# Relu² attention and a ReGLU feed-forward: another order for the loads and the attention pieces of the first two batches, a lag of 8 slots, and a one-piece last copy

## The chip, the cores and the metric

The kernel runs on one core of a Trainium2 chip. The metric is the device time of the kernel in microseconds (us). The time before is 423.1 us, the median of 4 runs (422.57 to 424.98).

## The reference

Inputs are q, k, v of shape (8, 12, 448, 64), w_gate and w_val of (768, 1536) and w_out of (1536, 768), all float32; the output has 3584 rows (8 batches of 448 tokens) of 768 columns, float32.

```python
scores = scale * np.matmul(q, k.transpose(0, 1, 3, 2))
attn = np.maximum(scores, 0.0) ** 2 / S
attn_out = np.matmul(attn, v)
x = attn_out.transpose(0, 2, 1, 3).reshape(B * S, H * D)
gate = np.maximum(x @ w_gate, 0.0)
val = x @ w_val
out = gate * val @ w_out
```

## The kernel before

**Data.** Every load is a DMA that POOL (GpSimd) issues (L329, in `dma_in`); it turns float32 into bf16 on the way, and all products are bf16 with float32 sums. The weights stay in SBUF: w_gate and w_val in six column pieces of 256 (`wg0..5`, `wv0..5`, 384 KB each as bf16), w_out in two column halves (`wo0`, `wo1`, 1152 KB each). The list LOADS (L906) sets the order of the loads of batches 0 and 1 and of all weights. In it `k0404` means k of batch 0 from head 4 on, 4 heads; `a` and `b` are the last 3 and the first 4 of the seven row tiles of q; `q` is both; `v` is v; `I` makes the identity matrix; `g3` is wg3 and wv3; `o1` is wo1. POOL issues a load only when the load eight places before it has landed, by the planner's reckoning.

**Attention.** For batches 0 and 1 q and k are turned on TensorE (`turn`, L444; transposes L460 into `t_ps`, copied to `qkT` by VectorE or ScalarE, L466 and L468). From batch 2 on the DMA transposes them (L501). Heads are taken in three groups of four. A piece of scores is four to eight 64x64 matmuls into `s_ps` (L591, L599 for the odd seventh key tile), then relu on ScalarE or VectorE (L609, L611), the square on VectorE (L628) and the product with v (L649), whose sum is copied to `xT` (L679, L681). Batch 0 is done in two parts of query rows, 192 (A) and then 256 (B), so that work can start early.

**Feed-forward.** For 128 columns of d_ff at a time, a gate product `g_ps` and a value product `v_ps` of six steps of 128 each; ScalarE takes the relu of the gate (L808), VectorE multiplies (L815) and leaves `hT`. Then an output product `o_ps` for 128 tokens and half of the 768 columns, of twelve steps. The first 24 products of batch 0 use the full 128x128 array (L715). All later ones use 64x64 tiles (L725, `Product.piece`): the upper 64 rows of the array (row 0) and the lower 64 (row 1) run side by side, row 1 going over the same products LAG slots later (`chain_ops`, L731; a slot is one step of 64x64 tiles in both rows). Both rows add into one PSUM bank, so the first matmul of row 1 in a product must come after row 0's last of that chunk of six: `ordered` (L434, called in L722) puts a wait on TensorE itself there. Output products are copied out of PSUM (L859 on ScalarE, L861 on VectorE) and stored by SP (L891).

**Order.** A planner (`Planner`, `plan`) goes over the operations with a cost each, keeps a time for each engine and for the load queue (`dmaq`), and at each step emits the operation that can start first. Its times decide only the order in which each engine gets its instructions; on the chip semaphores keep the dependences. For the attention of batch 0 and the turns of it, a list written out by hand, ORDER (L959), stands in for a choice: `T1k` is the turn of k of group 1, `A21` score piece 1 of group 2 of part A, `XA1` and `YA1` the two halves of the product with v, and an `f` puts a piece into two single PSUM banks. Feed-forward products are fitted between. Before the first data, `idle(8)` in `first_zeros` (L954) issues idle matmuls of 128x512 zeros into `w_ps` (L442), and the planner adds more (`filler`, L105 to L117) where it sees a gap before 24 us.

**The end.** The very last half of the output, 64+64 rows by 384 columns, is copied in two pieces of 192 columns, one by ScalarE and one by VectorE (L865 to L867), and then stored by SP (64 rows) and by ScalarE's queue (the other 64).

Of the kernel before, what the change touches and what calls it, by code (L numbers as in the profile page):

```python
# [12 lines left out]
ET = mybir.EngineType  # L13

XBAR_FROM = 2
LAG = 9
CHUNK = 6
NFULL = 24
PACE = 1.3
# [19 lines left out]
class Op:  # L39
    def __init__(self, engs, emit, deps=(), alloc=(), reads=(), xfer=0.0, prio=1, delay=0.0, bias=0.4,  # L40
                 mode=None, late=(), n=0, pace=0.0):
        self.engs, self.emit, self.n = engs, emit, n
        self.pace, self.after, self.anchor, self.name = pace, None, False, None
        self.mode, self.late = mode, list(late)
        self.deps, self.alloc, self.reads = list(deps), list(alloc), list(reads)
        self.xfer, self.prio, self.delay = xfer, prio, delay
        self.bias = bias
        self.lat = 1.3
        self.start = self.end = None


class Planner:
# [4 lines left out]
    AHEAD = 0.1  # L57
    BLOCK, HELD, SKEW = 256, 412, 100
    GROUP, APART = 3, 1.0

    def __init__(self):
        self.t = {"POOL": 1.35}
        self.ops = []
        self.dmaq = 0.0
        self.landed = []
        self.mode = "F"
        self.count, self.fetched = 0, []
# [36 lines left out]
    def commit(self, op, s, e):  # L104
        if e == "PE" and self.filler and 3.0 <= self.t.get(e, 0.0) < 24.0:  # L105
            res, one, make = self.filler
            t = max(self.t[e], min(res.free, default=1e9) + self.LAT)
            one *= 2 if t < 6.0 else 1
            n = int((s - t - 0.35) / one)
            if n > 0:  # L110
                fill = make(n)
                self.mode = fill.mode
                fill.start, fill.eng, fill.end = t, e, t + n * one
                res.free.remove(min(res.free))
                res.free.append(fill.end)
                self.t[e] = fill.end
                self.ops.append(fill)  # L117
        op.start, op.eng = s, e
        d = op.engs[e]
        if e == "PE":  # L120
            if op.mode[0] != self.mode:
                d += self.SWITCH
            self.mode = op.mode[-1]
        if op.n:
            for i in range(op.n):
                self.count += 1
                if (self.count + self.SKEW) % self.BLOCK == 0:
                    t = max([s + d * i / op.n] + self.fetched[-1:])
                    self.fetched.append(t + (6.15 if self.dmaq > t + 4.0 else 2.2))
        self.t[e] = s + d  # L130
        op.end = s + d
        if op.xfer:
            if e == "POOL":
                self.dmaq = max(self.dmaq, op.end + op.lat) + op.xfer
                op.end = self.dmaq + 0.7
                self.landed.append(op.end)
            else:
                op.end += 2.0 + op.xfer
        for b in op.alloc:
            b.res.free.remove(min(b.res.free))  # L140
            b.last = op.end
        for b in op.reads:
            b.readers -= 1
            b.last = max(b.last, op.end)
            if b.readers == 0:
                b.res.free.append(b.last)
        self.ops.append(op)
# [101 lines left out]
def kernel(  # L249
# [28 lines left out]
    OH = d_model // 2  # L278
# [43 lines left out]
        nc.gpsimd.affine_select(out=ident, in_=ident, pattern=[[-1, 128]], compare_op=ALU.is_equal,  # L322
                                fill=0.0, base=0, channel_multiplier=1)

    def dma_in(dst, src, n_desc, kb, deps=(), alloc=(), rate=380.0, pace=0.0):
        def emit():
            if op.after is not None:
                follow(nc.gpsimd.nop().ins, op.after.name, "pace of the loads")
            nc.gpsimd.dma_start(out=dst(), in_=src)  # L329

        op = Op({"POOL": 0.55 + 0.00047 * n_desc + (0.1 if pace else 0.0)}, emit, deps=deps, alloc=alloc, xfer=kb / rate,
                pace=pace)
        op.lat = 0.75 if n_desc <= 128 else 1.3
        pool_ops.append(op)
        return op

# [32 lines left out]
    def load_heads(b, h0, n, what="kv", pace=0.0):  # L369
        if b not in bat:  # L370
            bat[b] = Batch()
            bat[b].buf = Buf(r_in, NT if b >= XBAR_FROM else (3 if b == 0 else 2) * NQ)
            bat[b].vbuf = Buf(r_v, NQ * len(PARTS(b)))
            bat[b].tbuf = Buf(r_xb, NQ * (2 * NC + 1) if b > 0 else NQ * (NC + 1) * len(PARTS(b)))
            bat[b].qk_op, bat[b].v_op = {}, {}
        st = bat[b]

        def tile_of(name, n):
            if not hasattr(st, name):
                setattr(st, name, inp.tile([128, H, n, D], BF16, name=name))  # L380
            return getattr(st, name)

        hs = slice(h0, h0 + n)
        if b < XBAR_FROM:
            pt = lambda x: x[b, hs].rearrange("(a c) (p t) d -> (c p) a t d", c=2, t=NT)
            dst = lambda w, t0, t1: tile_of("qk", NT).rearrange("p (w a) t d -> p w a t d", w=2)[:, w, h0 // 2:(h0 + n) // 2, t0:t1]
            for c, x, w, t0, t1 in (("k", k, 1, 0, NT), ("q", q, 0, 0, NT), ("a", q, 0, 0, QA), ("b", q, 0, QA, NT)):
                if c in what:
                    op = dma_in(lambda w=w, t0=t0, t1=t1: dst(w, t0, t1), pt(x)[:, :, t0:t1], 64 * n, 16 * (t1 - t0) * n, rate=380.0 if b else 300.0,
                                alloc=[st.buf] if h0 == 0 and c == "k" else [])  # L390
                    for h in range(h0, h0 + n):
                        st.qk_op[(c if c != "q" else "a", h)] = op
        else:
            rows = lambda x: x[b, hs].rearrange("h (p t) d -> p h t d", t=NT)
            if "k" in what:
                k_op = dma_in(lambda: tile_of("qk", NT)[64:128, hs], rows(k), 64 * n, 112 * n, rate=340.0, pace=pace,
                              alloc=[st.buf] if h0 == 0 else [])
                q_op = dma_in(lambda: tile_of("qk", NT)[0:64, hs], rows(q), 64 * n, 112 * n, rate=340.0, pace=pace)
                st.qk_op[h0] = (k_op, q_op)
        if "v" in what:  # L400
            for r in range(2):
                src = v[b, hs].rearrange("h (p t) d -> p h t d", t=NT)[:, :, NC * r:NC * r + NC + 1]
                op = dma_in(lambda r=r: tile_of("vv", NC + 1)[64 * r:64 * r + 64, hs], src, 64 * n, 64 * n,
                            alloc=[st.vbuf] if h0 == 0 and r == 0 else [], rate=340.0 if b else 300.0,
                            pace=pace)
                for h in range(h0, h0 + n):
                    st.v_op.setdefault(h, []).append(op)
# [31 lines left out]
    def idle(n):  # L439
        w_ps = bank("w_ps")  # L440
        for _ in range(n):
            nc.tensor.matmul(w_ps, lhsT=zeros[:, :128], rhs=zeros, start=True, stop=True)  # L442
# [288 lines left out]
    def chain_ops(prods):  # L731
# [17 lines left out]
        res = []  # L749
        for c in range(0, n + LAG, six):  # L750
            top = [slots[t] if t < n else None for t in range(c, c + six)]
            low = [slots[t - LAG] if 0 <= t - LAG < n else None for t in range(c, c + six)]
            work = [(u, l) for u, l in zip(top, low) if u or l]
# [75 lines left out]
    def ffn_prods(b):  # L829
# [12 lines left out]
        for ti in tiles:  # L842
# [3 lines left out]
            for hf in range(2):  # L846
# [3 lines left out]
                ps = prod.ps  # L850
# [11 lines left out]

                final = b == B - 1 and ti == 2 * NC
                last_half = final and hf == 1
                pieces = [(0, OH, {"ACT", "DVE"})]  # L865
                if last_half:
                    pieces = [(0, OH // 2, {"ACT"}), (OH // 2, OH // 2, {"DVE"})]  # L867
                if last_half:
                    ps.readers = 2
                done = []  # L870
                for c0, n, engs in pieces:
                    cost = {e: d for e, d in on_psum(n).items() if e in engs}
# [27 lines left out]
                elif hf == 1:  # L900
                    others.append(Op({"SP": 0.2}, lambda f=emit_store: f(0, d_model, both), deps=cps, reads=[obuf],
                                     xfer=1.5))
        return res


    LOADS = ("k0004 a0008 k0404 k0804 a0804 I v0004 b0804 v0804 v0404 b0004 b0404 g0 g1 g2 kqv1004 "  # L906
             "kqv1804 g3 g4 kqv1404 g5 o0 o1")
    for x in LOADS.split():
        if x == "I":
            id_op = Op({"POOL": 0.35}, identity)  # L910
# [42 lines left out]

    def first_zeros():  # L954
        nc.vector.memset(zeros, 0.0)
        idle(8)

    head = {"W": Op({"PE": 3.0}, first_zeros, mode="F", n=16)}
    ORDER = ("W A21f A11 A22f B22 A20f T2k B11f T0a A00 A02f A13f XB1 A01 A10f YA0 B01 B03 YA2 A23 "  # L959
             "XA1f A12f T2a A03f B02 T0k B10 B13 XB2f T0b B00f B21f B12f XA0 T2b XA2 T1k T1a YB0 YB1 "  # L960
             "XB0 YB2 B23 YA1 B20 T1b")
    names = ORDER.split()
    for x in range(NQ):
        for what in "kab":
# [8 lines left out]
    head = [head[x.rstrip("f")] for x in names]  # L973
# [5 lines left out]
    for b in range(1, B):  # L979
        for g in range(NQ):  # L980
            pt = Part(b, g, 0, S)
# [59 lines left out]
```

## Time and profile before

| | us |
|---|---|
| median of 4 runs | 423.1 |
| all runs | 424.98, 422.57, 423.28, 422.93 |
| the profiled execution's own time | 424.98 |
| its span in the profile | 423.3 |
| TensorE matmuls busy | 412.6 |
| ScalarE, VectorE, GpSimd busy | 240.2, 185.4, 72.8 |
| mean granted TensorE clock | 0.999 |

The profile is of one execution, the first of the four. Its times count from the start of the span. PE is TensorE's matmuls, PEld its weight loads, which run beside the matmuls; DVE is VectorE, ACT ScalarE, POOL GpSimd and SP SyncE. A queue with a q after its name (SPq, POOLq) issues DMAs. Matmuls are pipelined, so one that is listed with 0.35 us stands only some 0.05 us behind the one before it, four in a slot of 0.189 us; ends of matmuls are modelled. Where a row ends with `[1.37 <-DMA qk<-in_k_dram]`, the engine stood idle for 1.37 us before it and the load of k ended that.

### The profile page before, as it was taken

To read this page: it belongs to the slowest core of one execution; us is meant where nothing else is said; L and a number is where in the kernel's file an instruction comes from. 1 tells how busy PE (TensorE), PEld (TensorE's weight loads), DVE (VectorE), ACT (ScalarE), POOL (GpSimd) and SP (SyncE) were. 2 spreads that over 40 slices of the span, in tenths; PEclk is the share of its full clock that TensorE was granted. 3 is DMA by queue.
4 is the path that set the end of the run, shared out by engine and by line. 5 is a ranking of instruction groups with operands and counts; after the bars stand their busy time and mean duration, and the time that the engine had idled before them with its cause. 6 is when DMAs were issued, how large, how long until landed. Compare 5 with 4: busy or idle time off the path is not lost.

```text
span 423.3 us, 19116 instructions
## 1 busy us (share of the span) xinstructions
PE 412.6 (97%) x8847; PEld 373.6 (88%) x8847; DVE 185.4 (44%) x340; ACT 240.2 (57%) x362; POOL 72.8 (17%) x118
## 2 busy tenths in 40 slices
PE   7899899999999999999999999999999999999995
PEld 3577569988999889999999999999999999986695
DVE  1975555245632665354535345543533445102200
ACT  3973467457667776755567556774557655332221
POOL 7836510011005102400420122020000000000000
PEclk9999999999999999999999999999999999999999
DMA  8999999798299766959787986297003300040014
GB/s 110 180 199 198 199 205 196 116 152 125 38 141 183 133 81 90 167 120 125 104 114 134 158 118 85 31 155 139 4 2 77 77 3 4 5 111 3 3 41 113
DMA packets 77488, 44.88 MB, mean 106 GB/s; under 512 B 36832, under 2 KB 73952, under 8 KB 77408
## 3 DMA queue, kind: packets, MB, share of 16 engines
q0 software_dynamic: 39360, 24.39, 42.7%
q1 hardware_dynamic: 37968, 19.18, 25.0%
q8 instruction: 69, 1.13, 1.1%
q10 hardware_dynamic: 80, 0.10, 0.1%
q14 instruction: 11, 0.09, 0.1%
HBM read 48.76 MB, written 11.01 MB: 141 GB/s over the span
## 4 chain that ended last, share of the span: by engine, by line
PE 83%; DMA 12%; POOL 3%; issue 0%; DVE 0%; ACT 0%; POOLq 0%
PE o_ps L725 24%; PE v_ps L725 23%; PE g_ps L725 23%; PE s_ps L649 7%; PE s_ps L591 6%; DMA qk<-in_k_dram 5%; DMA wo<-in_moe_w_out_dram 5%; DMA wv<-in_moe_w_val_dram 3%; POOL wg L329 1%; PE s_ps L599 1%; POOL qk L329 1%; POOL wv L329 1%; POOL vv L329 0%; DVE o_sb L861 0%; ACT o_sb L859 0%
## 5 line engine op out<-in xcount | busy, mean ns | idle before, releaser
L725 PE MATMUL g_ps<-xT,wg 64*64 64x448 bf16 x2160 | 205.8, 349 | 0.0
L725 PE MATMUL v_ps<-xT,wv 64*64 64x448 bf16 x2160 | 194.6, 349 | 0.0
L609 ACT ACTIVATE r_sb<-s_ps 128x896 bf16<-128x896 f32 (+4 forms) x173 | 149.8, 882 | 73.6 <-PE s_ps L591 57.8
L725 PE MATMUL o_ps<-wo,hT 64*64 64x384 bf16 x2688 | 146.7, 323 | 0.4 <-DVE qkT L468 0.3
L628 DVE TENSOR_TENSOR at<-r_sb 128x896 bf16<-128x896 bf16 (+3 forms) x163 | 99.8, 617 | 105.2 <-ACT r_sb L609 105.0
L725 PEld LDWEIGHTS <-wg 64*64 64x64 bf16 x2160 | 135.5, 107 | 9.9
L725 PEld LDWEIGHTS <-wv 64*64 64x64 bf16 x2160 | 131.8, 107 | 10.3
L725 PEld LDWEIGHTS <-hT 64*64 64x64 bf16 x2688 | 131.9, 107 | 2.6 <-DMA wo<-in_moe_w_out_dram 0.5
L815 DVE TENSOR_TENSOR hT<-v_ps,g_sb 128x448 bf16<-128x448 f32 (+2 forms) x102 | 60.9, 597 | 101.0 <-PE v_ps L725 91.9
L591 PE MATMUL s_ps<-qkT 64*64 64x448 bf16 (+2 forms) x648 | 82.7, 330 | 0.7 <-ACT r_sb L609 0.5
L808 ACT ACTIVATE g_sb<-g_ps 128x448 bf16<-128x448 f32 (+2 forms) x102 | 53.0, 519 | 51.2 <-PE g_ps L725 44.9
L649 PE MATMUL s_ps<-at,vv 64*64 64x448 bf16 (+2 forms) x672 | 49.5, 339 | 0.2 <-ACT r_sb L609 0.2
L591 PEld LDWEIGHTS <-qkT 64*64 64x64 bf16 x648 | 42.7, 106 | 4.5 <-issue 2.4
L859 ACT ACTIVATE o_sb<-o_ps 128x384 f32<-128x384 f32 (+1 forms) x56 | 27.8, 496 | 23.9 <-PE o_ps L725 23.5
L649 PEld LDWEIGHTS <-vv 64*64 64x64 bf16 x756 | 36.5, 107 | 2.4 <-issue 1.3
L329 POOL DMA_DIRECT2D vv<-in_v_dram x44 | 27.5, 630 | 52.6 <-PE s_ps L649 12.9
L679 ACT CAST xT<-s_ps 128x896 bf16<-128x896 f32 (+2 forms) x24 | 20.8, 865 | 23.4 <-PE s_ps L649 23.2
L922 POOL COPY mark<-qkT 64x1 bf16<-64x1 bf16 x5 | 0.9, 181 | 124.4 <-DMA qkT<-spare 124.4
L329 POOL DMA_DIRECT2D qk<-in_k_dram x24 | 15.6, 649 | 18.0 <-ACT g_sb L808 10.3
L329 POOL DMA_DIRECT2D qk<-in_q_dram x26 | 17.1, 657 | 8.8 <-ACT r_sb L609 3.2
L599 PE MATMUL s_ps<-qkT 64*64 64x448 bf16 (+2 forms) x108 | 16.1, 329 | 0.0
L490 DVE COPY spare<-qk 128x768 bf16<-128x768 bf16 x42 | 12.5, 354 | 0.0
(31 smaller groups left out, 97.5 us busy)
## 6 DMA issues: line engine op xcount, KB each, us to landing
out_dram<-o_sb SPq DMA_DIRECT2D x54, 192.0 KB, 3.5
qk<-in_k_dram POOLq DMA_DIRECT2D x24, 224.0 KB, 5.6
vv<-in_v_dram POOLq DMA_DIRECT2D x42, 128.0 KB, 5.6
qk<-in_q_dram POOLq DMA_DIRECT2D x21, 224.0 KB, 6.0
wg<-in_moe_w_gate_dram POOLq DMA_DIRECT2D x6, 384.0 KB, 10.5
wv<-in_moe_w_val_dram POOLq DMA_DIRECT2D x6, 384.0 KB, 11.1
wo<-in_moe_w_out_dram POOLq DMA_DIRECT2D x2, 1152.0 KB, 16.9
vv<-in_v_dram POOLq DMA_DIRECT2D x2, 384.0 KB, 12.1
```

What stands on the lines that cost most here:

```text
L329: nc.gpsimd.dma_start(out=dst(), in_=src)
L490: nc.vector.tensor_copy(box["p"][:, :, s], st.qk[:, :, t, :].rearrange("p (a c) d -> p a c d", c=2))
L591: nc.tensor.matmul(half_of(h2)[o:o + P2, m * n:(m + 1) * n], lhsT=kq(1, j, h2, key_off(b) + c * 128 + o, P2), rhs=kq(0, j, h2, self.c0, n) ...
L599: nc.tensor.matmul(half_of(u)[o:o + 64, :n], lhsT=kq(1, j, h2, key_tail(b), P2), rhs=kq(0, j, h2, self.c0, n), start=True, stop=True)
L609: o.name = nc.scalar.activation(dst, src, AF.Relu).ins.name
L628: lambda: nc.vector.tensor_tensor(self.at_tile(i), loc["r"][:, :2 * ne], loc["r"][:, :2 * ne], ALU.mult),
L649: ins = nc.tensor.matmul(x_of(slice(64 * h2, 64 * h2 + 64), j), lhsT=st.vv[p, 4 * g + 2 * j + h2, NC * (1 - row) if tail else c + row, :], ...
L679: nc.scalar.copy(dst, src)
L725: ins = nc.tensor.matmul(self.out()[c], lhsT=self.weights(p, k)[:, c], rhs=self.moving(p, k), start=(row == 0 and k == 0), stop=(row == 1 ...
L808: nc.scalar.activation(loc["gs"], gp.out(), AF.Relu)
L815: nc.vector.tensor_tensor(hs["hT"][:, mf, t0:t0 + n], vp.out(), loc["gs"], ALU.mult)
L859: nc.scalar.activation(out=dst, in_=src, func=AF.Copy, scale=float(out_scale))
```

## The change

It does six things:

1. LOADS has another order. Among others, q's last tiles of heads 8–11 come first, v of batch 0 is loaded after all its k, and of batch 1 the heads 8–11 come between wo0 and wo1, where they stood before wg3.
2. ORDER, the hand-written order of the turns, score pieces and v products of the head, is another.
3. The planner's model of the load queue is another: a load is counted as slower by 0.95 us for each instruction block that is fetched while the queue has not run empty, the first 9.2 us go at 0.64 of the rate, and small loads of batch 0 have an allowance (`skew`).
4. LAG is 8, was 9.
5. `idle(WARMUP)` with WARMUP = 7 takes the place of `idle(8)`, and its planned cost of 3.0 becomes 1.25 + 0.425 · 7; the filler's matmuls count double before 4.7 us, not before 6.0.
6. The last half of the last output tile is copied in one piece of 384 columns on VectorE.

```diff
-LAG = 9
+LAG = 8
+WARMUP = 7
...
-            one *= 2 if t < 6.0 else 1
+            one *= 2 if t < self.WARM else 1
...
             if e == "POOL":
-                self.dmaq = max(self.dmaq, op.end + op.lat) + op.xfer
-                op.end = self.dmaq + 0.7
+                if op.end + op.lat > self.dmaq + self.lag:
+                    self.drained = op.end + op.lat
+                t, work = max(self.dmaq, op.end + op.lat), op.xfer
+                slow = min(work, max(0.0, self.COLD - t) * self.COLD_RATE)
+                self.dmaq = t + slow / self.COLD_RATE + work - slow
+                self.lag = 0.95 * sum(1 for f in self.fetched if self.drained < f < self.dmaq)
+                op.end = self.dmaq + self.lag + 0.1 + op.skew
...
-        op = Op({"POOL": 0.55 + 0.00047 * n_desc + (0.1 if pace else 0.0)}, emit, deps=deps, alloc=alloc, xfer=kb / rate,
+        op = Op({"POOL": 0.62 + 0.00045 * n_desc + (0.1 if pace else 0.0)}, emit, deps=deps, alloc=alloc, xfer=kb / rate,
                 pace=pace)
-        op.lat = 0.75 if n_desc <= 128 else 1.3
+        op.lat = 0.75
+        op.skew = skew
...
-                pieces = [(0, OH, {"ACT", "DVE"})]
-                if last_half:
-                    pieces = [(0, OH // 2, {"ACT"}), (OH // 2, OH // 2, {"DVE"})]
-                if last_half:
-                    ps.readers = 2
+                pieces = [(0, OH, {"DVE"} if last_half else {"ACT", "DVE"})]
...
-    LOADS = ("k0004 a0008 k0404 k0804 a0804 I v0004 b0804 v0804 v0404 b0004 b0404 g0 g1 g2 kqv1004 "
-             "kqv1804 g3 g4 kqv1404 g5 o0 o1")
+    LOADS = ("a0804 k0004 I a0004 k0404 a0404 k0804 v0804 v0008 b0804 b0008 g0 g1 kqv1004 g2 g4 "
+             "kqv1404 g3 g5 o0 kqv1804 o1")
...
-        idle(8)
-
-    head = {"W": Op({"PE": 3.0}, first_zeros, mode="F", n=16)}
-    ORDER = ("W A21f A11 A22f B22 A20f T2k B11f T0a A00 A02f A13f XB1 A01 A10f YA0 B01 B03 YA2 A23 "
-             "XA1f A12f T2a A03f B02 T0k B10 B13 XB2f T0b B00f B21f B12f XA0 T2b XA2 T1k T1a YB0 YB1 "
-             "XB0 YB2 B23 YA1 B20 T1b")
+        idle(WARMUP)
+
+    head = {"W": Op({"PE": 1.25 + 0.425 * WARMUP}, first_zeros, mode="F", n=2 * WARMUP)}
+    ORDER = ("W YA0 B22f T1a A21f A20 T0k A10 T2a T0b A03 A01 T0a XA2f B03 B10f A22 XA1 B12 B00f YB0 "
+             "B02f A02 XB1 A11 T2b A12f T1k A23f B23 B13f T2k B21 B11 XA0f B20f YB2 YA2 XB0f XB2 A00f "
+             "A13f T1b YB1 YA1 B01")
```

Both ORDER lists name the same operations; an operation that cannot start yet is passed over for the next that can.

More of the change, by code (lines that the diff above doesn't have):

```diff
@@ L47, in __init__ @@
         self.bias = bias
-        self.lat = 1.3
+        self.lat, self.skew = 1.3, 0.0
         self.start = self.end = None
@@ L59 @@
     GROUP, APART = 3, 1.0
+    COLD, COLD_RATE = 9.2, 0.64
+    WARM = 4.7
     def __init__(self):
@@ L63, in __init__ @@
         self.ops = []
-        self.dmaq = 0.0
+        self.dmaq = self.lag = self.drained = 0.0
         self.landed = []
@@ L323, in identity, with dma_in @@
                                 fill=0.0, base=0, channel_multiplier=1)
-    def dma_in(dst, src, n_desc, kb, deps=(), alloc=(), rate=380.0, pace=0.0):
+    def dma_in(dst, src, n_desc, kb, deps=(), alloc=(), rate=380.0, pace=0.0, skew=0.0):
         def emit():
@@ L388, in load_heads @@
                 if c in what:
-                    op = dma_in(lambda w=w, t0=t0, t1=t1: dst(w, t0, t1), pt(x)[:, :, t0:t1], 64 * n, 16 * (t1 - t0) * n, rate=380.0 if b else 300.0,
+                    op = dma_in(lambda w=w, t0=t0, t1=t1: dst(w, t0, t1), pt(x)[:, :, t0:t1], 64 * n, 16 * (t1 - t0) * n, rate=380.0,
+                                skew=0.8 if b == 0 and t1 - t0 < 4 else 0.0,
                                 alloc=[st.buf] if h0 == 0 and c == "k" else [])
@@ L392, in load_heads @@
                         st.qk_op[(c if c != "q" else "a", h)] = op
+                        if c == "q":
+                            st.qk_op[("b", h)] = op
         else:
@@ L403, in load_heads @@
                 op = dma_in(lambda r=r: tile_of("vv", NC + 1)[64 * r:64 * r + 64, hs], src, 64 * n, 64 * n,
-                            alloc=[st.vbuf] if h0 == 0 and r == 0 else [], rate=340.0 if b else 300.0,
+                            alloc=[st.vbuf] if h0 == 0 and r == 0 else [], rate=340.0 if b > 1 else 380.0,
                             pace=pace)
```

## Prediction

> **What bounds the kernel now.** I read the share of the span and the chain that ended last first, then TensorE's waits, then its rows around each wait.
>
> ```profile
> PE 412.6 (97%) x8847; PEld 373.6 (88%) x8847; DVE 185.4 (44%) x340; ACT 240.2 (57%) x362; POOL 72.8 (17%) x118
> ...
> PE 83%; DMA 12%; POOL 3%; issue 0%; DVE 0%; ACT 0%; POOLq 0%
> ```
>
> TensorE is busy 412.6 of 423.3 us, so about 10.7 us at most are idle, and the chain is TensorE except for a transfer part early. Where that part ends is seen in the chain cut to 30–70 us (columns: start, length, what):
>
> ```profile
> 34.64 12.17 DMA wv<-in_moe_w_val_dram
> 46.81 0.28 issue
> 47.10 19.18 DMA wo<-in_moe_w_out_dram
> 66.27 0.04 issue
> 66.32 0.35 PE o_ps L725 x2
> ```
>
> The last weight load, wo1 (second half of w_out), is issued at 47.10 and lands at 66.3; from there the chain is TensorE alone. By stretches of the profile TensorE is busy 33.68 of 33.70 us from 66.3 to 100, and all of every 100 us to 400. So the end is **66.3 us plus the TensorE work that stands after wo1's first use**. Time won before 66.3 counts only if wo1 lands earlier, or if more work has been put ahead of it. TensorE's waits (us in total, times, longest), matmuls first and weight loads after:
>
> ```profile
> PE t_ps L460 <- DMA qk<-in_k_dram: 2.6, 3, 1.4
> PE w_ps L442 <- DVE zeros L955: 1.3, 1, 1.3
> PE v_ps L715 <- DMA wv<-in_moe_w_val_dram: 0.6, 1, 0.6
> PE s_ps L591 <- ACT r_sb L609: 0.5, 1, 0.5
> ...
> PEld L725 <- DMA wo<-in_moe_w_out_dram: 0.5, 1, 0.5
> ```
>
> TensorE stands only 0.5 us at wo1; the largest wait is 1.4 us for a k load:
>
> ```profile
> 47.94 0.58 PE L460 MATMUL t_ps<-ident,qk 128*64 128x128 bf16 x14 [1.37 <-DMA qk<-in_k_dram]
> ```
>
> That is the transposes of batch 1's second head group (heads 4–7), whose k lands at 47.9 because heads 8–11 are loaded first.
>
> **When wo1 lands after the change.** From the issue rows and their times to landing, loads never stop between 2.9 and 66.3 us, at about 192 KB/us: at 30.55 us 4416 KB have landed, at 54.4 8832, with wo0 9984 at 60.2, with wo1 11136 at 66.3. The instruction queue (q8) fetches 8 blocks of 16 KB in that time, about 0.95 us each on one of the 16 engines, which the loads there wait behind. The new list moves k, q, v of heads 8–11 of batch 1 to between wo0 and wo1, but the same 11136 KB come before wo1's end. I take 66.3 again. One fetch less would give 65.35, one more 67.25. POOL issues the same loads in another order, two DMAs fewer; it is busy 2.9 of the first 4 us, and waits 0.5 and 2.0 us at the two wo loads for room in its queue, so it is no bound there.
>
> **What is ahead of wo1's first use.** I counted the matmuls in TensorE's order in both kernels up to that product, and multiplied by the spacing in before's rows (64x448: four in 0.189 us, so 0.0472 each; 64x384 0.0406; transposes 0.0362; 64x192 0.0205; 64x256 0.0272; 128x192 0.0848; 128x256 0.1093). Before: 370×0.0472 + 12×0.0406 + 168×(0.0362+0.0205+0.0272) + 72×(0.0848+0.1093) = 46.0 us. After: the same but 388 of 64x448, 18 more, 16 of them scores of batch 1: 46.9 us. So if wo1 lands at 66.3 and TensorE is there in time, **0.85 us less is left behind it: −0.85**.
>
> **Is TensorE there in time?** Clock less work done is what TensorE has lost. Before: 16.1 us at 33.3, 16.6 at 43.6, 17.8 at 46.6, 19.2 after the stall at 47.9, 19.9 at 64.7. After, by bytes: k0 lands at 6.3 us, k1 9.9, k2 11.6, v of heads 0–7 at 15.7, wv2 34.1, then heads 4–7 of batch 1 at 39.2–41.8, k of heads 8–11 at 57.8. The transposes of k1 now stand ahead of the first scores, which start about 10.4 us instead of 8.4; v at 15.7 costs 0.4, and TensorE meets wv2 at 34.1 with 17.0 us done: lost 17.1, one more than before there. The 1.37 us stall goes: 28 us of work lie ahead of those transposes, which puts them near 45, over 5 us after their k; the last group's come at 41 us of work, about 59.5 and so 1.5 after theirs. What is late next is wo1. If before's other losses after 33.3 recur whole (0.5+1.2+0.7), TensorE arrives at 46.9+17.1+2.4 = 66.4. Following the new order wait by wait with before's durations, I find 1.4–1.7 in place of 2.4: 65.4–65.7. So it comes 0.9 early to 0.1 late; I take in time, as three of the four losses summed belong to waits for DVE and ACT that the new order spaces apart.
>
> **Warm-up.** In before 13 idle matmuls of 512 columns take
>
> ```profile
> 1.26 5.46 PE L442 MATMUL w_ps<-zeros 128*128 128x512 bf16 x13 [1.26 <-DVE zeros L955]
> ```
>
> about 0.42 us each, and 14 transposes at 6.65 take 0.58 in all. After: 7 of them, ending near 4.25, then gaps until k lands. The granted clock reads 1.00 from the start, so it doesn't show this slow phase; the speed-up near 6.3 us is read from spacing alone. If it comes as early as in before, it costs nothing; if only at 16.5 us, the roughly 4 us of work until then doubles, partly into idle, and by following the order TensorE reaches wo1 0.7–1.0 later, 66.1–66.7: 0 to 0.4 lost. I count 0, since the nearest row (speed-up 5 us after the start) is still met by the seven and the first transposes. The Trainium skill, "TensorE: Matmul & The Clock Gate", Part 1 (The HAM clock gate), says that the clock stays at half until one free-running window of about 3.4 us was busy, and that the phase differs by run: this speaks against shortening the warm-up to 3.0 us. By that rule the sum would lose up to 0.4 of its 1.0 and show more spread; the 5.0 us that before's row took is less than two such windows.
>
> **LAG 8.** In a chained product row 1 follows row 0 by LAG slots, and its first weight load waits for row 0's last matmul: 180 such waits in gate and value products, 112 in output products. In before the weight load starts 0.22 us after the modelled end of the matmul it waits for. One slot less (0.189) leaves 0.03. What a wait of TensorE on itself takes:
>
> ```profile
> 14.83 0.52 PE L649 MATMUL s_ps<-at,vv 64*64 64x192 bf16 x16 [0.17 <-ACT r_sb L609]
> ...
> 15.42 0.36 PE L649 MATMUL s_ps<-at,vv 64*64 64x192 bf16 x8
> ```
>
> The second starts 0.07 after the first's end (15.35). So a weight load may come 0.04 late; but it starts 0.19 ahead of its matmul and takes 0.107, so 0.08 is spare. Behind it stand both rows' further weight loads and matmuls, so an uncovered 0.04 would be paid 292 times. I take covered: 0. One slot less at the end of the last chain (0.1625): **−0.16**.
>
> **One-piece last copy.** The end of before:
>
> ```profile
> 417.96 2.53 SPq L891 DMA_DIRECT2D out_dram<-o_sb  x4
> ...
> 418.88 0.33 ACT L859 ACTIVATE o_sb<-o_ps 128x192 f32<-128x192 f32 x1 [0.43 <-PE o_ps L725]
> 419.24 0.36 DVE L861 TENSOR_SCALAR o_sb<-o_ps 128x192 f32<-128x192 f32 x1 [15.27 <-ACT o_sb L859]
> 419.63 0.56 ACTq L891 DMA_DIRECT2D out_dram<-o_sb  x1
> ```
>
> The two pieces run one after the other, until 419.60. One piece on DVE, twice the columns, lies between 0.36 and 0.72, near 0.56: until 419.45. But SP's queue is busy with the previous issue until 419.84, its last store issues at 419.94 and lands last, at 422.26. So 0 (−0.15 if the queue is free sooner, +0.1 if the copy takes 0.72). From batch 2 on the order is the same: 0.
>
> **Sum.** The profiled execution took 424.98 (1.7 us around its span): 424.98 − 0.85 − 0.16 = 423.97. It lies 1.9 above the median of 423.1, so on the median: **422.1 us**.
>
> **Rivals.**
> 1. *TensorE late at wo1* (slow clock until 16 us, or other waits in the head). For: arrival by before's losses is 66.4, and the first scores start 2 us later. Against: followed wait by wait, 0.6–0.9 is spare. From 0.5 to 3 us later than 65.7 gives 422.3–424.5; above 1.0 us over 66.3 the gain is gone.
> 2. *wo1 lands earlier* (a fetch less, looser queue), and TensorE decides, at 65.4 or before. Gain 0.85+0.16+0.7 to 1.6: 421.4–420.5. For: TensorE is early. Against: same bytes, more instructions ahead of wo1.
> 3. *Lag 8 stalls, slower.* Place: row 1's first weight load, L725. Price 0.04 each: 4.5 us if only the 112 output products pay (426.6), 11.7 if all do (433.8). It decides once the wait takes over 0.03+0.08 = 0.11 after the modelled end. For: the margin shrinks to 0.03 and ends are modelled. Against: the 0.07 of the row above.
> 4. *The order doesn't do what it says*: wo1 0.85 later, or the extra scores not ahead of it; only the lag gains: 422.9.
>
> **How the numbers follow.** Forecast 0.50 (422.1, its own range 421.4–423.0), rival 1 0.20, rival 2 0.15, rival 3 0.11, rival 4 0.04. Over 0.5% (2.1 us, about what a measurement here can tell from no change) faster means below 421.0: most of rival 2 with a little of the forecast's edge, 0.13. Slower means above 425.2: rival 3 and the end of rival 1, 0.14. Same 0.73. Range 420.4 (rival 2's end) to 424.4 (rival 1's end); rival 3 and some tails are left out.
>
> **What would show it.** wo1's landing near 66.3 and the chain passing from it into TensorE; no wait at the second group's transposes; a value-product wait until about 34.1; the slot still 0.189 and 0.1625 us in the steady stretches and TensorE busy all of 100–400; the last SP store still held by its queue. wo1 landing before 65.4 with TensorE waiting for something else, or a slot grown in chained products, would make me wrong.

## The result, and the profile after

The changed kernel takes 423.9 us in the median (35 runs, 422.94 to 425.66), the kernel before 423.0 (55 runs, 422.06 to 425.03, in a comparison of the two). The ratio is **1.0021, interval 1.0013 to 1.0028**: 0.9 us slower, where 1.0 us faster was forecast. (One run of before, of 874.86 us, is left out.)

The profiled execution of the changed kernel took 423.58 us, its span is 421.6. That is 1.7 us *less* than the span of the profile that the prediction was made from, though the medians stand the other way round. So one of the two profiles is not a usual one. The profile after, first the busy time and the chain that ended last:

```profile
PE 410.8 (97%) x8848; PEld 309.5 (73%) x8848; DVE 189.3 (45%) x348; ACT 235.8 (56%) x352; POOL 71.7 (17%) x116
...
PE 90%; DMA 8%; POOL 1%; issue 0%; DVE 0%; SPq 0%; POOLq 0%; DVEq 0%
```

The chain is TensorE for 90%, not 83%, and the transfer of wo1 is gone from it. Where it was, in the chain cut to 30 to 70 us (start, length, what), stands this:

```profile
21.70 11.71 DMA wv<-in_moe_w_val_dram
33.46 0.67 PE v_ps L727 x6
34.13 0.49 PE g_ps L727 x6
```

From wv2's landing at 33.4 on the chain is TensorE but for two pieces: a copy of `qkT` on VectorE (0.64 us at 59.3), and, as the last thing that TensorE waited for, a DMA transpose for batch 2:

```profile
82.18 5.40 DMA qkT<-spare
```

wo1 landed at 64.51. The first product with it (its weights are a piece of `hT`) started at 65.36:

```profile
65.19 0.12 PEld L737 LDWEIGHTS <-hT 64*64 64x64 bf16 x2
...
65.36 0.35 PE L737 MATMUL o_ps<-wo,hT 64*64 64x384 bf16 x2
```

There is no idle time before that row: TensorE comes 0.85 us after the load. Its longest waits in the whole span are these (us in total, times, longest):

```profile
PE t_ps L472 <- DMA qk<-in_q_dram: 1.5, 1, 1.5
PE w_ps L454 <- DVE zeros L963: 1.3, 1, 1.3
PE t_ps L472 <- DMA qk<-in_k_dram: 1.1, 2, 0.7
PE s_ps L611 <- ACT r_sb L621: 0.5, 1, 0.5
PE s_ps L603 <- ACT r_sb L621: 0.5, 2, 0.3
PE v_ps L737 <- DVE qkT L480: 0.3, 1, 0.3
PE v_ps L727 <- DMA wv<-in_moe_w_val_dram: 0.3, 1, 0.3
```

The wait of 1.4 us at the second group's transposes of batch 1 is gone, as forecast; the waits for q and k are now ahead of 10 us.

**A measure for what follows.** From the rows of one profile I take the start of each matmul and subtract the work of all matmuls before it, at the spacings that the prediction used (idle matmuls count as none). That is the time that TensorE has *lost* up to a given amount of work, and it can be compared between orders.

### The profile page after: what moved, and what is told of

It is laid out like the page before. It is cut to its first block, busy times and chain, and to the rows that moved or that the text cites. A ratio compares the mean times of both kernels' runs of the same rounds, so it can differ in the third digit from the quotient of the medians.

```text
span 421.6 us, 19123 instructions
## 1 busy us (share of the span) xinstructions
PE 410.8 (97%) x8848; PEld 309.5 (73%) x8848; DVE 189.3 (45%) x348; ACT 235.8 (56%) x352; POOL 71.7 (17%) x116
## 4 chain that ended last, share of the span: by engine, by line
PE 90%; DMA 8%; POOL 1%; issue 0%; DVE 0%; SPq 0%; POOLq 0%; DVEq 0%
PE o_ps L737 26%; PE v_ps L737 25%; PE g_ps L737 23%; PE s_ps L661 7%; PE s_ps L603 6%; DMA wv<-in_moe_w_val_dram 5%; DMA qk<-in_k_dram 1%; DMA qkT<-spare 1%; PE v_ps L727 1%; PE g_ps L727 1%; PE s_ps L611 1%; POOL qk L337 1%; PE t_ps L472 0%; POOL wg L337 0%; DVE qkT L480 0%
## 5 line engine op out<-in xcount | busy, mean ns | idle before, releaser
L737 PE MATMUL o_ps<-wo,hT 64*64 64x384 bf16 x2688 | 141.8, 323 | 0.0
L737 PEld LDWEIGHTS <-wv 64*64 64x64 bf16 x2160 | 103.7, 107 | 34.7 <-issue 0.3
L737 PEld LDWEIGHTS <-wg 64*64 64x64 bf16 x2160 | 103.9, 107 | 34.0
L737 PEld LDWEIGHTS <-hT 64*64 64x64 bf16 x2688 | 116.8, 107 | 7.8
L603 PE MATMUL s_ps<-qkT 64*64 64x448 bf16 (+2 forms) x648 | 62.9, 330 | 1.0 <-ACT r_sb L621 0.5
L661 PE MATMUL s_ps<-at,vv 64*64 64x448 bf16 (+2 forms) x644 | 42.6, 341 | 0.0
L871 ACT ACTIVATE o_sb<-o_ps 128x384 f32<-128x384 f32 x50 | 24.8, 500 | 24.7 <-PE o_ps L737 24.7
L691 ACT CAST xT<-s_ps 128x896 bf16<-128x896 f32 (+1 forms) x23 | 20.2, 878 | 23.1 <-PE s_ps L661 23.1
L661 PEld LDWEIGHTS <-vv 64*64 64x64 bf16 x756 | 26.5, 107 | 7.3 <-issue 0.6
L603 PEld LDWEIGHTS <-qkT 64*64 64x64 bf16 x648 | 23.7, 106 | 8.5 <-issue 2.6
```

The costliest lines, as they stand in the source:

```text
L603: nc.tensor.matmul(half_of(h2)[o:o + P2, m * n:(m + 1) * n], lhsT=kq(1, j, h2, key_off(b) + c * 128 + o, P2), rhs=kq(0, j, h2, self.c0, n) ...
L661: ins = nc.tensor.matmul(x_of(slice(64 * h2, 64 * h2 + 64), j), lhsT=st.vv[p, 4 * g + 2 * j + h2, NC * (1 - row) if tail else c + row, :], ...
L691: nc.scalar.copy(dst, src)
L737: ins = nc.tensor.matmul(self.out()[c], lhsT=self.weights(p, k)[:, c], rhs=self.moving(p, k), start=(row == 0 and k == 0), stop=(row == 1 ...
L871: nc.scalar.activation(out=dst, in_=src, func=AF.Copy, scale=float(out_scale))
```

## Experiments

The theories: **A**, the kernel before is bound by wo1's landing in its usual executions too, but that landing is near 64.5, and the changed kernel's TensorE comes later than that since its head lost time; **B**, lag 8 costs; **C**, the one-piece copy costs.

### 1. The kernel before, profiled again

The kernel is unchanged.

> The kernel before, unchanged, for a second profile. Theory A (late head): the profiled execution that I read was 1.9 us above the median because of two waits, 1.37 us for k of heads 4-7 of batch 1 and 0.53 us for wo1; a usual execution has neither. So span 421.0 to 421.6, wo1 landing at 64.3 to 65.0, the wait at the second head group's transposes under 0.4 us, no wait of a weight load for wo, and TensorE at the first wo1 product at 64.2 to 64.8. Theory B (the lag costs) and theory C (the copy costs): the profile is like the first, span 422.5 to 423.5, wo1 at 66.3, the 1.4 us wait there again.

423.19 us, span 421.5. Its waits:

```profile
PE t_ps L460 <- DMA qk<-in_k_dram: 1.5, 3, 0.9
...
PE o_ps L725 <- DMA wo<-in_moe_w_out_dram: 0.6, 1, 0.6
...
PEld L725 <- DMA wo<-in_moe_w_out_dram: 1.0, 1, 1.0
```

and the two rows that matter:

```profile
45.88 0.58 PE L460 MATMUL t_ps<-ident,qk 128*64 128x128 bf16 x14 [0.38 <-DMA qk<-in_k_dram]
...
64.76 0.35 PE L725 MATMUL o_ps<-wo,hT 64*64 64x384 bf16 x2 [0.60 <-DMA wo<-in_moe_w_out_dram]
```

The span and the landing are as theory A had them: the wait for k is 0.38, not 1.37, and wo1 lands at 64.72, not 66.27. One part missed: TensorE still waits for wo1, 0.60 us. Experiments 3 and 14 below, whose order is that of before up to there, agree (the last two rows are the changed kernel, the second of experiment 10):

| profile | wo1 lands | first wo1 product | work ahead | lost |
|---|---|---|---|---|
| before, the one read | 66.27 | 66.32 | 46.02 | 20.30 |
| before again | 64.72 | 64.76 | 46.02 | 18.74 |
| one-piece copy | 64.00 | 64.05 | 46.02 | 18.03 |
| before, short warm-up | 64.03 | 64.07 | 46.02 | 18.05 |
| changed | 64.51 | 65.36 | 46.87 | 18.49 |
| changed again | 65.00 | 65.86 | 46.87 | 18.99 |

The old order starts that product within 0.1 us of the landing, the new one 0.85 and 0.86 after it. The last column's mean is 18.27 for the three usual profiles of before and 18.74 for the changed kernel.

### 2 to 4. The lag, the copy, and the change without both

**Experiment 2**, in the kernel before:

```diff
-LAG = 9
+LAG = 8
```

> The kernel before with LAG 8 alone. Theory A: one slot less at the end and no stall, ratio 0.9990 to 1.0002 (-0.16 us by itself); the slot stays 0.189 us. Theory B: the +0.9 us of the change come from here, ratio 1.0020 or more. Theory C: 0.9996, like A.

Ratio 1.0009, interval 0.9996 to 1.0023: no difference shown, and 0.9 us is within it. The trace is finer. From the 13th output matmul (the first with wo1) to the last matmul's start it has 351.80 us, against 351.96 in each of the three usual profiles of before's order: the slot of 0.16 gained, no stall.

**Experiment 3**, in the kernel before:

```diff
-                pieces = [(0, OH, {"ACT", "DVE"})]
-                if last_half:
-                    pieces = [(0, OH // 2, {"ACT"}), (OH // 2, OH // 2, {"DVE"})]
-                if last_half:
-                    ps.readers = 2
+                pieces = [(0, OH, {"DVE"} if last_half else {"ACT", "DVE"})]
```

> The kernel before with the one-piece last copy alone; every other instruction as before. Theories A and B: 0 by SP's queue, ratio 0.9996 to 1.0004. Theory C: the copy of 0.56 us and one less queue cost 0.4 us or more, ratio 1.0010 or more.

Ratio 1.0004, 0.9994 to 1.0013: no difference shown, theory C has no support.

**Experiment 4**:

```diff
 the changed kernel with
-LAG = 8
+LAG = 9
 and the two-piece copy
```

> The changed kernel with LAG 9 and the two-piece copy again, so that only the loads' order, the head's order, the planner's model and the warm-up are changed. Theory A: the whole loss and the lag's 0.16 more: ratio 1.0020 to 1.0030, TensorE at the first wo1 product near 66.0 without a wait for it. Theories B and C: at or under 1.0000, as the loss is taken away.

Ratio 1.0050, 1.0031 to 1.0068: slower still, so the lag and the copy do not carry the loss, but it is 1 us more than A gave. The planner makes another order with lag 9, and in it TensorE stands once near 290 us:

```profile
PE g_ps L737 <- issue: 1.0, 1, 1.0
```

for nothing that the profile shows; an instruction fetch at 278 took 2.60 us there in place of the usual 0.95. That the fetch causes the wait is argued, not shown. wo1 is first used at 66.20, 1.00 after its landing and without a wait for it, as in the changed kernel; 19.42 us are lost by then.

### 5 and 6. 224 KB more ahead of wo1, in both kernels

```diff
+    scrap = const.tile([128, 2, NT, D], BF16)
...
-        wo_op[c] = dma_in(lambda: w_out_sb[c], wo[:, :, c * OH:(c + 1) * OH], 1536, 2160)
+        def dst():
+            if c == 1:
+                nc.gpsimd.dma_start(out=scrap, in_=k[7, 8:12].rearrange("(a c) (p t) d -> (c p) a t d", c=2, t=NT))
+            return w_out_sb[c]
+
+        wo_op[c] = dma_in(dst, wo[:, :, c * OH:(c + 1) * OH], 1536, 2160)
```

**Experiment 5**, in the kernel before:

> The kernel before with one more load of 224 KB, which nobody reads, right ahead of wo1 in the queue; every other instruction and order as before. In the second profile of before TensorE stood 0.6 us at wo1, which landed at 64.7. So here, by theory A (before is bound by wo1's landing, after by TensorE's arrival): wo1 about 1.15 us later, and the time 0.9 to 1.3 us longer, ratio 1.0021 to 1.0031. If before was bound by TensorE too: under 0.5 us, ratio under 1.0012.

Ratio 1.0032, 1.0020 to 1.0043, that is 1.4 us: wo1 landed at 65.34, and TensorE waited for it:

```profile
65.38 0.35 PE L731 MATMUL o_ps<-wo,hT 64*64 64x384 bf16 x2 [1.47 <-DMA wo<-in_moe_w_out_dram]
```

So before is bound there, and nothing after it gives the time back.

**Experiment 6**, in the changed kernel:

> The changed kernel with the same useless 224 KB right ahead of wo1. In its profile wo1 landed at 64.5 and TensorE used it first at 66.04 without a wait. Theory A: wo1 at 65.7, still in time, so 0 to 0.2 us over the changed kernel: ratio to before 1.0017 to 1.0028, and no wait of 0.3 us or more for wo. If the changed kernel is bound by wo1 in its usual executions: 1.15 us over it, ratio 1.0044 to 1.0054.

Ratio 1.0039, 1.0026 to 1.0053: between the two expectations, so the time decides nothing. The profile has wo1 at 65.79, its first product at 66.47, and no wait for it; TensorE was late by itself. (The 66.04 in the expectation is 65.36 in the trace.) Experiment 9 asks the same the other way round.

### 7. Thirteen idle matmuls in the changed kernel

```diff
-WARMUP = 7
+WARMUP = 13
```

> The changed kernel with 13 idle matmuls ahead in place of 7. If the short warm-up costs the head (the clock's speed-up comes late in many executions, as in the profile of the kernel with lag 9, where 14 transposes still took 0.96 us at 12.4): 0.4 to 0.9 us back, ratio to before 0.9998 to 1.0012, and 14 transposes at full rate (0.58 us) by 10 us. If the head loses by its waits for loads alone: ratio 1.0018 to 1.0026, as the changed kernel.

Ratio 1.0035, 1.0019 to 1.0050: nothing came back. In its profile the transposes run at full rate from 6.56 us on (20 in 0.75 us; 14 in 0.58 at 9.46) and yet 15.87 us are lost at 8 us of work, as the first transposes wait for q and k (1.9 and 0.9 us).

### 8. The late loads alone in the kernel before

```diff
-             "kqv1804 g3 g4 kqv1404 g5 o0 o1")
+             "g3 g4 kqv1404 g5 o0 kqv1804 o1")
```

> The kernel before with the late part of the new loads alone: k, q, v of heads 8-11 of batch 1 between wo0 and wo1, so heads 4-7 are loaded earlier; the first 17 loads, the head's order, lag 9, the warm-up and the copy as before. 374 in place of 370 of the 64x448 matmuls stand ahead of wo1's first use (-0.19 us if wo1 sets the end). Theory A: the stall at the second head group's transposes goes (0.3 to 0.4 us in usual executions, 1.4 in the one I read), wo1 stays the bound: ratio 0.9985 to 1.0000. If what I forecast for the change held for the late loads (0.85 us): 0.9980. If the late loads are what costs: 1.0010 or more.

Ratio 1.0002, 0.9991 to 1.0013: a little above what theory A gave, with an interval that reaches into it. The stall at the second group's transposes is gone from its profile, and TensorE waits for wo1 instead (0.8 us at the weight load, until the landing at 63.84): the time won is given back at the next late load.

### 9 to 11. w_out in parts, and the changed kernel again

```diff
-        wo_op[c] = dma_in(lambda: w_out_sb[c], wo[:, :, c * OH:(c + 1) * OH], 1536, 2160)
+        h = KF // 2
+        wo_op[c, s] = dma_in(lambda: w_out_sb[c][s], wo[:, s * h:s * h + h, c * OH:(c + 1) * OH], 768, 1080)
...
 in the changed kernel:
-kqv1404 g3 g5 o0 kqv1804 o1
+kqv1404 g3 g5 o00 kqv1804 o10 o01 o11
 in the kernel before, with LAG = 8:
-kqv1804 g3 g4 kqv1404 g5 o0 o1
+g3 g4 kqv1404 g5 o00 o10 kqv1804 o01 o11
```

An output product then waits for the second part of its half from its seventh step on only.

**Experiment 9**, the changed kernel with parts:

> The changed kernel with w_out loaded in the same two parts, so wo1's first part lands about 3 us earlier. Theory A (the changed kernel is bound by TensorE's arrival): no gain, ratio to before 1.0014 to 1.0028. If it is bound by wo1's landing: 0.9995 to 1.0008.

**Experiment 10**, the changed kernel as it is:

> The changed kernel unchanged, beside these on one chip and for a second profile. Theory A: ratio 1.0013 to 1.0028, no wait for wo1, TensorE has lost 14.8 to 16 us when 8 us of its work are done, and 0.3 to 0.4 us between 65 and 70 us of work, at the first scores of batch 2. Rival (its first profile was a lucky one in another way): a wait of 0.5 us or more for wo1.

Beside each other on one chip: 1.0018 (1.0004 to 1.0032) with parts, 1.0024 (1.0012 to 1.0036) without. wo1's first part landed at 58.39 and not at 65.00, and its first product started at 65.50 and not 65.86. Both ratios lie where theory A put them: the changed kernel is not bound by wo1. One part missed: between 65 and 70 us of work experiment 10 lost 0.15 us, not 0.3 to 0.4.

**Experiment 11**, the kernel before with parts, the late loads of experiment 8 and lag 8:

> The kernel before with the new late loads, lag 8 and both halves of w_out loaded in two parts of six steps each (first parts ahead of heads 8-11 of batch 1, second parts after). In before TensorE stood 0.5 to 1.0 us at wo1 in four profiles of its order; the parts land by 54 and by 64, TensorE needs them at 62 and from 65 on. Theory A (before is bound by wo1's landing): the wait goes, 0.6 to 1.0 us and the lag's 0.16 gained, ratio 0.9974 to 0.9986. If wo1's landing doesn't bind before: 0.9995 to 1.0005.

Ratio **0.9982, 0.9970 to 0.9994**: 422.63 us beside 423.02, the one version here that is faster than both kernels. wo1's first part landed at 54.59, and TensorE's rows hold no wait for wo. The late loads and the lag alone gave 1.0002 and 1.0009 (experiments 8 and 2). So the parts gain in the old head and not in the new one, as theory A says.

### 12 to 14. The old head, and all without the new one

**Experiment 12**:

```diff
 in the changed kernel:
-"a0804 k0004 I a0004 k0404 a0404 k0804 v0804 v0008 b0804 b0008 g0 g1 kqv1004 g2 g4 "
+"k0004 a0008 k0404 k0804 a0804 I v0004 b0804 v0804 v0404 b0004 b0404 g0 g1 g2 kqv1004 g4 "
 and ORDER as before
```

> The changed kernel with the old order of the first loads (up to g2) and the old head order; the late loads stay new (heads 8-11 of batch 1 between wo0 and wo1), lag 8, one-piece copy, the new planner model and warm-up stay. Ahead of wo1's first use stand 45.9 us of work. If the new head's order and first loads are what costs: TensorE has lost 12.5 to 13.7 us when 8 us of its work are done (14.8 to 15.9 in the changed kernel's profiles, 12.5 to 13.0 in those of before), is at wo1 before it lands, and the ratio to before is 0.9990 to 1.0010. If the loss comes from the model, the lag or the copy: 1.0018 or more, as the changed kernel.

Ratio 1.0063, 1.0044 to 1.0082: by its bound (1.0018 or more) the second expectation, but far above the changed kernel, so it doesn't tell the two apart. The old lists under the new model of landings do not give the old order; 16.96 us are lost at 8 us of work. A list and the model that it was made with go together.

**Experiment 13**, the kernel before with the late loads (experiment 8), LAG = 8 (2) and the one-piece copy (3):

> The change without its head: the kernel before with the new late loads, lag 8 and the one-piece copy; first loads, head order, planner model and warm-up as before. If the head is what makes the change slower: TensorE has lost 12.5 to 13.2 us at 8 us of work, and the ratio to before is 0.9985 to 1.0003 (0.16 us by the lag and up to 0.28 by six more score matmuls ahead of wo1). If the late loads, the lag and the copy cost when put together: 1.0015 or more.

Ratio 1.0011, 1.0001 to 1.0021: above what was expected. In its profile the head is the old one (13.38 lost at 8 us of work), wo1 landed at 65.10 and TensorE waited 0.7 us for it; in experiment 8, with the same loads, it landed at 63.84. By themselves the three parts gave 1.0002, 1.0009 and 1.0004, none clear of 1. So up to half of the 0.9 us may not be the head's, and why wo1 lands at 63.8 in one profile of these loads and at 65.1 in the other is open.

**Experiment 14**:

```diff
 in the kernel before:
-            one *= 2 if t < 6.0 else 1
+            one *= 2 if t < 4.7 else 1
...
-        idle(8)
+        idle(7)
-    head = {"W": Op({"PE": 3.0}, first_zeros, mode="F", n=16)}
+    head = {"W": Op({"PE": 4.225}, first_zeros, mode="F", n=14)}
```

> The kernel before with 9 idle matmuls ahead of the first transposes in place of 13 (11 in place of 15 in all); the order behind them is the same. In three of five profiles with 7 idle matmuls 14 transposes took 0.96 us at 9.5 to 10.1 us; in all profiles with 13 they took 0.58 by 7 us. If the short warm-up leaves the clock slow: 14 transposes at 0.96 us after 8 us in the profile; TensorE loses 0.5 to 1.5 us of its head, of which wo1's wait hides 0.5 to 1.0, so ratio 1.0000 to 1.0015. If the warm-up's length doesn't matter: 0.58 us by 7 us, ratio 0.9995 to 1.0005.

Ratio 0.9999, 0.9991 to 1.0008: in the old head the shorter warm-up costs nothing; its profile was at full rate by 5.47 us.

### 15 to 17. Why the head loses

**Experiment 15**:

```diff
 in the changed kernel:
-"a0804 k0004 I a0004 k0404
+"k0004 a0004 I a0804 k0404
```

> The changed kernel with k and q of heads 0-3 as first loads and the q tiles of heads 8-11 third; by the planner the first 20 score matmuls then stand ahead of the second group's transposes. If it is the order of the first loads that delays the head: first scores at 7.5 to 8.3 us (10.3 in the changed kernel), 13 to 14.3 us lost at 8 us of work, and the ratio to before falls from 1.0021 to 0.9995 to 1.0012. If the head loses elsewhere (the clock, or waits behind the first scores): 1.0015 to 1.0030.

Ratio 1.0027, 1.0018 to 1.0037. The first scores came at 7.8 us and not at 10.3, but 15.39 us were lost at 8 us of work all the same: TensorE then waits for q and k of the other groups (1.7 and 1.2 us). My reason, that the transposes of k1 ahead of the first scores are the loss, falls.

**Experiment 16**:

```diff
 in the changed kernel:
-                                skew=0.8 if b == 0 and t1 - t0 < 4 else 0.0,
+                                skew=0.9 if b == 0 else 0.0,
...
-                            pace=pace)
+                            pace=pace, skew=0.9 if b == 0 else 0.0)
```

> The changed kernel, whose planner reckons every load of batch 0 as landing 0.9 us later (the new model's landings lie 0.1 to 1.4 us before those of the profiles up to 18 us); loads and head list unchanged. The plan then sets the first 20 score matmuls ahead of the second group's transposes. If the head loses because its order was planned for earlier landings: first scores at 7.5 to 8.8 us (10.3 in the changed kernel), 0.5 us or more less lost at 16 us of work than the 15.4 to 17 of the new head, and the ratio to before at 0.9998 to 1.0014. If the loss isn't in that mismatch: 1.0018 to 1.0032.

Ratio 1.0036, 1.0024 to 1.0049. The first scores came near 9.4 us, later than expected, and 17.27 us were lost at 16 us of work: no better than the new head as it was. So it is not the mismatch either, as far as a shift by 0.9 us can show it.

**Experiment 17**:

```diff
 in the changed kernel, in place of the new lines on t, slow and lag:
+                self.dmaq = max(self.dmaq, op.end + op.lat) + op.xfer
+                op.end = self.dmaq + 0.7
```

> The changed kernel with the old model of the load queue in its planner (landings from 8 us on reckoned later); loads, head list, lag, warm-up and copy as changed. If the new model's early landings cost: ratio to before 0.9998 to 1.0014, as with the later landings. If the new lists cost by themselves: 1.0018 to 1.0032.

Ratio 1.0154, 1.0135 to 1.0173. TensorE arrives at the first output product at 68.4 (64.0 in the changed kernel). Like experiment 12, it shows that model and lists cannot be exchanged singly.

## Why the prediction was wrong

**The step that failed: "I take 66.3 again".** The bytes ahead of wo1 are the same, and that reasoning held; the number came from an execution that was 1.9 us over its median and whose loads were late: wo1 landed 1.6 to 2.3 us after its usual time. Usual landings are 64.0 to 64.7 in the kernel before and 64.5 and 65.0 in the changed one. (That its two waits, 1.37 us for k and 0.53 us for wo1, add up to 1.90 proves nothing: usual executions wait there too, 0.38 and 0.60 us in experiment 1.) The prediction then took the 1.9 off at the end to come to the median, but left the landing, on which the sum rested, where it was: with wo1 at 64.5 to 65.0 and TensorE at 65.4 to 65.9, the second is the bound, and that is rival 1, TensorE late at wo1. By its picture, wo1 early and TensorE deciding at 65.4, it is rival 2 as well; but that rival's gain took before's wo1 to stay at 66.3, and before's usual landing is as early.

**The arrival was right.** Forecast were 65.4 to 65.7, or 66.4 if before's other losses recur; measured 65.36 and 65.86. Part of that is luck: at wv2 16.4 and 16.8 us were lost, not 17.1, and from there to wo1 2.1 and 2.2, not 1.4 to 1.7. Against a landing of 64.5 the forecast's own numbers give rival 1: 65.4 − 46.9 = 18.5 lost, against 64.3 − 46.0 = 18.3 before.

**The sum as measured.** The −0.85 for more work ahead of wo1 became +0.5 (18.74 against 18.27 in the table). The lag's −0.16 is there in the trace. "From batch 2 on the order is the same: 0" was wrong by 0.15 to 0.39: the first scores of batch 2 wait for their transposed q and k,

```profile
87.62 0.11 PEld L603 LDWEIGHTS <-qkT 64*64 64x64 bf16 x4 [0.49 <-DMA qkT<-spare]
```

and in the changed kernel the lost time rises from 18.76 to 19.15 between 65 and 70 us of work (19.26 to 19.41 in the second profile); in the usual profiles of before it does not rise there. 0.47 − 0.16 + 0.27 is 0.6 of the 0.9 us; these five profiles differ by 0.7 in their mean spans (421.8 and 421.1).

**The other steps.** The second group's transposes no longer wait: right. The value product waits for wv2, until 33.46 (34.1 forecast): right in the first profile; in the second there is no such wait. Lag 8 causes no stall: right, TensorE is busy 100.00 of every 100 us from 100 to 400. The copy: right, 0; the new one took 0.56 us, the estimate. What the traces show as worse is the head: at 8 us of work 14.8 to 15.7 us are lost in the changed kernel's two profiles, 12.7 to 13.0 in the three usual ones of before. At wv2, near 33.4 us, it is 16.4 and 16.8 against 14.8 to 15.0, 1.4 to 2.0 more; the prediction had 17.1 against 16.1, one more, as it took before's 16.1 from the one execution that it read.

**What stays open.** Why the new head loses 2 to 3 us by 8 us of work is not settled: first loads, warm-up, a shift of the reckoned landings and the old model each brought nothing back. The traces show one thing beside it that the experiments did not separate. The queue of loads is slower at first with the new list: by 12 us it had moved 1.32 and 1.28 MB in the changed kernel's two profiles, 1.48 to 1.51 in the three usual ones of before; by 60 us it is still behind, 10.76 and 10.70 against 10.89 to 10.93, which at 0.195 MB/us is 0.7 to 1.2 us. It cannot be all: experiment 12, with the old first loads, had moved 1.50 by 12 us and yet lost 16.96 us by 8 us of work. The late execution first read shows the same sign: 2.83 MB by 20 us, where the three usual ones had 3.01 to 3.05, and 10.70 by 60; what held its loads back in those 20 us is not known, nor how much of the 0.9 us is scatter of wo1's landing (experiment 13's 1.0011 without the new head).

## What to carry to other kernels

Before a profile is taken as the baseline, compare its own time with the median: if it lies well above, look what was late in it (here the loads, wo1 by 1.6 to 2.3 us), and do not build the forecast on that. A gain in one wait counts only up to the next late load or engine; here two kernels whose heads differ by 2 to 3 us after 8 us of work differ by some 0.5 at the first product of wo1, since the one that is ahead then meets longer waits, the last of them for wo1. A load that binds can be split by when its parts are needed: with the late loads and the lag that gave 0.9982, where reordering the head gave a loss.

## What was not expected of the hardware

With seven idle matmuls the slow phase of TensorE at the start ends at very different times. This is the changed kernel with w_out in parts, 14 transposes at 9.87 us:

```profile
9.87 0.96 PE L473 MATMUL t_ps<-ident,qk 128*64 128x128 bf16 x14
...
15.03 1.02 PE L455 MATMUL w_ps<-zeros 128*128 128x512 bf16 x4
```

and this the changed kernel's second profile:

```profile
6.98 0.58 PE L472 MATMUL t_ps<-ident,qk 128*64 128x128 bf16 x14 [1.85 <-DMA qk<-in_k_dram]
...
9.50 0.96 PE L472 MATMUL t_ps<-ident,qk 128*64 128x128 bf16 x14
...
12.04 0.58 PE L472 MATMUL t_ps<-ident,qk 128*64 128x128 bf16 x14
```

Fast at 6.98, slow again at 9.50, fast at 12.04. The granted clock shows the slow phase in the second of these profiles and not in the first. In the second it reads 0.50 from 7.97 to 11.38; in the 3.41 us before that, which hold the wait of 1.85 us, it reads 1.00, and TensorE was busy 1.56 us of them. In the first it reads 1.00 from 4 to 13 us, through the slow rows.

In the changed kernel's first profile they took 0.58 from 5.72 on, while with 13 idle matmuls the 14 transposes took 0.58 from 5.6 to 6.9 us on in every profile of before's order. Of the five profiles of the changed kernel with seven (its own two and those of experiments 4, 6 and 9), four have 14 transposes at 0.96 us between 9.5 and 10.1; the expectation of experiment 14 counts three. At 10 us of work the fast profile had lost 15.08 us, the two shown here 15.83 and 15.95, but the one with 13 idle matmuls, at full rate from 6.56 on, 16.34. So what a slow phase costs there is not separated from the waits for loads. The rule of the Trainium skill that the prediction weighed ("TensorE: Matmul & The Clock Gate", Part 1: The HAM clock gate; half rate until one free-running window was busy, a phase that differs by run) agrees with slow phases that end at different times; whether it gives each of these ends, no run here shows. A cost to the median was not found: 13 idle matmuls in the new head gained nothing (experiment 7).
